# Two loading queues at the start of a fused attention and MLP block: other pieces, other order

## The chip, the cores and the metric

The kernel runs on one core of one Trainium2 chip. A core has five engines with a queue of instructions each: TensorE (PE) for matrix products, ScalarE (ACT), VectorE (DVE), GpSimd (POOL) and SyncE (SP). Transfers from memory are issued here by SP (queue q1 in the profile, "the sync queue") and by ACT (queue q10, "the scalar queue"). The metric is the time on the device in microseconds; lower is better. The median of five runs before the change is 158.0 us (157.48 to 158.24).

## The reference

All inputs are bf16. x has 2048 tokens of 448 features. The output is the sum of x, a linear attention of the normalised x, and a two-layer perceptron of the normalised x:

```python
xn  = layernorm(x)
qkv = (xn @ wqkv)                      # 16 heads of 28
phi = concat(softmax(q @ w_phi), softmax(-q @ w_phi))   # the same for k
kv  = phi_k^T v ;  z = sum over s of phi_k
o   = (phi_q kv) / (phi_q z + 1e-6)
out = x + o @ wo + silu(xn @ w1) @ w2  # w1: 448 x 1792, w2: 1792 x 448
```

## The kernel before, in words

The tokens are 16 tiles of 128, `t` 0 to 15, in four chunks of four tiles. `x_sb[:, t]` holds tile t. The contraction of 448 is cut into 7 slices of 64 rows, and every matrix product is issued as a pair on the lower and the upper half of PE's rows (`LO`, `HI`).

Every operation is first recorded in a list (`_Prog.op`, L167) with an estimated duration and the memory it reads and writes. A planner (`schedule`, L199; `_pass`, L229) then gives each engine its order. PE's order is the order of the program. Operations recorded with `ordered=True` also keep the program's order on their engine, and all loads are of that kind. The others are placed by estimated start and due time; `eng_free` (L254) says from when an engine is free. `emit_engine` (L961) writes the engines' instructions with semaphore waits, each engine working strictly through its list. So an instruction that waits holds up all behind it on its engine, and a transfer that waits holds up all transfers behind it on its queue.

The start goes as follows.

- POOL makes an identity matrix; PE multiplies it with itself (`warm`, L474), 32 + 4 pairs, before there is data. ACT loads its table for Silu with a dummy activation (L471).
- SP issues loads of x0, x1, the lower half of w1's first piece, x2 and x3 as one load, the lower halves of w1's second and third piece, then wqkv's columns for q and k (`wraw`, loads "wqk0" and "wqk1") and for v. ACT issues the upper halves of w1's three pieces and then four small loads of w_phi into `BD`. `load_w1` (L493) cuts w1 at columns 256, 512 and 896 of each half.
- Layernorm of a tile: statistics on DVE (`LN_st`, L533), aggregation on DVE and the power -1/2 on POOL (`LN_ag`, L538), the scaled copy `xnd` on DVE (`LN_b`, L547). Tiles 0 to 3 are then transposed on PE (`X_tr`, L572) and evicted to `xT`, one half by ACT and one by DVE (`X_ev`, L578). Tiles 4 to 11 are transposed by DMA transposes on the sync queue (`X_dma`, L562).
- `F1p` (L601) and `F1` (L589) are the first layer of the perceptron: a pair of 128-row tiles of the hidden layer, over 128 or more tokens, then Silu on ACT. Tile 0 and 1 start with `F1p`; then `F1(0, i, 0, 2)` for i from 2 to 6 does the other hidden tiles for tiles 0 and 1, with `X_tr` of tiles 2 and 3 in between, and `F1(0, i, 2, 2)` does all of them for tiles 2 and 3.
- `FT_tr` (L762) and `FM` (L785) multiply w_phi into the q and k weights on PE, from `wraw` and `BD`.
- `phase_e(0)` (L869) is then V and QK of the first chunk, with two second-layer tiles as fillers, `F2_early(f2[0])` and `F2_early(f2[1])`. After it, chunk 1's first layer, `F1(1, i, 0, 4)`, reads the transposes of tiles 4 to 7.
- Later loads carry `after=`, an instruction of PE that has to be over first. The loads of x8 to x11 and x12 to x15 wait for the end of `QK(0)`:

```python
QK(0)
mk = P.ops[P.last[("pe", "o")]]
QK(1)
F2_early(f2[0])
load_x(8, 12, after=mk)
load_x(12, 16, after=mk)
```

On the sync queue they come before the four transposes of tiles 4 to 7 (L567), and the first transpose of `phT` (L638) comes behind those.

Of the kernel before, what the change touches and what calls it, by code (L numbers as in the profile page):

```python
# [8 lines left out]
ACTF = mybir.ActivationFunctionType  # L9
# [129 lines left out]
class _Prog:  # L139
# [89 lines left out]
    def _pass(self, when):  # L229
        ops = self.ops  # L230
        n = len(ops)
        lat = self.lat
        tend = max(when.values()) + 3000.0
        for o in reversed(ops):
            if o.eng == "pe":
                o.alap = when[o.id]
                continue
            m = tend
            for u in o.users:
                uu = ops[u]  # L240
                if u in o.odeps:
                    continue
                m = min(m, uu.alap - (lat(o, uu) if o.id in uu.deps else 0.0))
            extra = 0.0
            if o.is_dma:
                extra = o.fixed if o.fixed is not None else 1200.0 + o.nbytes
            o.alap = m - o.dur - extra

        ndeps = [len(o.deps) + len(o.odeps) for o in ops]
        ready = {e: set() for e in ENGINES}  # L250
        for o in ops:
            if ndeps[o.id] == 0:
                ready[o.eng].add(o.id)
        eng_free = {"pe": 800.0, "act": 2100.0, "dve": 800.0, "pool": 800.0, "sp": 800.0}  # L254
        act_table = [None]
        dma_free = [0.0]
        order = {e: [] for e in ENGINES}
        done = 0
        WAIT_TOL = 60.0

        def est(o):
            t = eng_free[o.eng]
            for d in o.deps:
                dd = ops[d]
                t = max(t, dd.end + lat(dd, o))
            for d in o.odeps:
                t = max(t, ops[d].end if not ops[d].is_dma else ops[d].start + ops[d].dur)
            if o.eng == "act" and o.table is not None and act_table[0] is not None and o.table != act_table[0]:
                t += 1300.0
            return t  # L270

        while done < n:
            best = None
            for e in ENGINES:
                if not ready[e]:
                    continue
                c = [(est(ops[i]), ops[i]) for i in ready[e]]
                t0 = min(x[0] for x in c)
                t, o = min(((t, o) for t, o in c if t <= t0 + WAIT_TOL), key=lambda x: (x[1].alap, x[1].id))
                for t2, o2 in c:  # L280
                    if o2 is o or o2.alap >= o.alap or t2 >= t + o.dur:
                        continue
                    la = max(t - o.alap, t + o.dur - o2.alap, 0.0)
                    lb = max(t2 - o2.alap, t2 + o2.dur - o.alap, 0.0)
                    if lb < la - 1.0:
                        t, o = t2, o2
                if best is None or t < best[0]:
                    best = (t, o)
            assert best is not None, "scheduler deadlock"
            t, o = best  # L290
            ready[o.eng].discard(o.id)
            o.start = t
            if o.is_dma:
                issue_end = t + o.dur
                eng_free[o.eng] = issue_end
                if o.fixed is not None:
                    o.end = t + o.fixed
                else:
                    x0 = max(issue_end + 900.0, dma_free[0])
                    dma_free[0] = x0 + o.nbytes  # L300
                    o.end = dma_free[0] + 300.0
            else:
                o.end = t + o.dur
                eng_free[o.eng] = o.end + (0.0 if o.eng == "pe" else 30.0)
                if o.eng == "act" and o.table is not None:
                    act_table[0] = o.table
            order[o.eng].append(o.id)
            done += 1
            for u in o.users:
                ndeps[u] -= 1  # L310
                if ndeps[u] == 0:
                    ready[ops[u].eng].add(u)
        return order, max(o.end for o in ops)


def bass_parallel_sum__linear_kernel_hedgehog__dense_activation_silu__prompt_kernel(
# [21 lines left out]
    with es:  # L338
# [65 lines left out]
        P = _Prog()  # L404
# [54 lines left out]
        def load(dst, src, nbytes, run, name, eng="sp", issue=650.0, after=None):  # L459
            return P.dma(lambda e: e.dma_start(out=dst, in_=src), service(nbytes, run), writes=[dst], name=name, eng=eng,  # L460
                         issue=issue, ordered=True, after=after)
# [6 lines left out]
        P.op("pool", 230, lambda e: e.memset(ones_bf[:], 1.0), [], [ones_bf[:]], name="ones", ordered=True)  # L468
        P.op("pool", 290, lambda e: e.affine_select(ident[:], ones_bf[:], [[1, 128]], ALU.is_equal, 0.0, base=0,
                                                    channel_multiplier=-1), [ones_bf[:]], [ident[:]], name="ident", ordered=True)  # L470
        P.op("act", 220, lambda e: e.activation(tabw[:], neghalf[:], ACTF.Silu), [neghalf[:]], [tabw[:]],  # L471
             table="silu", name="tab", ordered=True)

        def warm(n, sl=2, d=55.5):  # L474
            for i in range(n):
                pair([(bank(2 * sl + q)[:, 0:128], ident[HALF[q], :], ident[HALF[q], :], True, True) for q in range(2)],
                     128, "warm", dur=d)

        P.unit = "warm"
        warm(32, d=107.0)  # L480
        warm(4)


        xv = A_x[0].rearrange("(p t) d -> p t d", t=NT)
        ov = out[0].rearrange("(p t) d -> p t d", t=NT)

        def load_x(t0, t1, after=None):
            load(x_sb[:, t0:t1, :], xv[:, t0:t1, :], (t1 - t0) * 128 * D * 2, (t1 - t0) * D * 2, f"x{t0}", issue=430, after=after)

        w1v = B_w1.rearrange("(s p) f -> p s f", p=64)  # L490
        W1S = [0, 256, 512, 896]
# [1 line left out]
        def load_w1(i):  # L493
# [2 lines left out]
            load(w1_sb[LO, :, a:b], w1v[:, :, a:b], n, (b - a) * 2, f"w1l{i}")  # L496
            load(w1_sb[HI, :, a:b], w1v[:, :, 896 + a:896 + b], n, (b - a) * 2, f"w1h{i}", eng="act")

        load_x(0, 1)
        load_x(1, 2)  # L500
        load_w1(0)
        load_x(2, 4)
        load_w1(1)
        load_w1(2)
        load(wraw[:, 0:3, 8:904], A_wqkv[0:384, 0:896].rearrange("(b p) c -> p b c", p=128), 384 * 896 * 2, 1792, "wqk0")
        load(wraw[LO, 3, 8:904], A_wqkv[384:448, 0:896], 64 * 896 * 2, 1792, "wqk1")
        P.op("pool", 300, lambda e: e.memset(BD[:], 0.0), [], [BD[:]], name="bd0", ordered=True)
        for p0 in (0, 904):
            P.op("pool", 150, lambda e, p0=p0: e.memset(wraw[:, :, p0:p0 + 8], 0.0), [], [wraw[:, :, p0:p0 + 8]],
# [23 lines left out]
        def LN_st(t, od=False):  # L533
            P.unit = f"LN{t}"
            xs = x_sb[:, t, :]
            P.op("dve", 630, lambda e: e.bn_stats(st6[:, t, :], xs), [xs], [st6[:, t, :]], name="bnst", ordered=od)  # L536
# [41 lines left out]
        def X_ev(t, sl, qs=(0, 1), od=False):  # L578
            P.unit = f"X{t}"
            j = t % 4  # L580
            for q in qs:
                src = bank16(2 * sl + q)[:, 0:448].rearrange("p (s n) -> p s n", s=NS)
                dst = xT[:, 0, :, j * 128 + q * 64:j * 128 + (q + 1) * 64]
                if q == 0:
                    act(dst, src, ACTF.Identity, 448, name="xT_ev")
                else:
                    P.op("dve", 390, lambda e, dst=dst, src=src: e.tensor_copy(dst, src), [src], [dst], name="xT_ev", ordered=od)  # L587
# [227 lines left out]
        X_tr(0, s0, HS, NS)  # L815
        X_ev(0, s0, (0, 1), True)
        LN_b(1, PARTS[1:], True)
        LN_st(2, True)
        P.unit = "warm"
        warm(10)  # L820
        give(s0)
# [1 line left out]
        def x1():  # L823
            X_tr(1, s1, 0, HS)
            X_tr(1, s1, HS, NS)
            X_ev(1, s1, (0, 1), True)
            LN_ag(2, True)
            LN_st(3, True)
            LN_ag(3, True)
            LN_b(2, od=True)  # L830
            LN_b(3, od=True)
            pads_init()
# [36 lines left out]
        def phase_e(c, f2):  # L869
            t = 4 * c  # L870
            if c == 0:
                V(0, lambda: FM(2))
                V(2, lambda: FM(3))
                QK(0)
                mk = P.ops[P.last[("pe", "o")]]
                QK(1)
                F2_early(f2[0])
                load_x(8, 12, after=mk)
                load_x(12, 16, after=mk)
                QK(2)  # L880
                QK(3)
                F2_early(f2[1])
                pend.extend((0, 1, 2, 3))
                return
            QK(t)
            mk = P.ops[P.last[("pe", "o")]]
            if c == 1:
                for s in range(NS):
                    for q in range(2):
                        load(wo_sb[HALF[q], s, :], wov[s], 64 * D * 2, 896, f"wo{s}", after=mk)  # L890
            F2_early(f2[0])
            QK(t + 1)
            V(t)
            kv(2)
            QK(t + 2)
            F2_early(f2[1])
            QK(t + 3)
            kv(2)
            V(t + 2)
            pend.extend((t, t + 1, t + 2, t + 3))  # L900
# [138 lines left out]
```

## Time and profile before

| | before |
|---|---|
| median of five runs | 158.0 us |
| the profiled execution, its own time | 157.97 us |
| its span in the profile | 156.2 us |
| PE busy (2298 matmuls) | 144.4 us, 92% of the span |
| DVE, ACT, POOL busy | 94.0, 93.4, 83.6 us |
| transfers of q1 (sync), q10 (scalar) | 15.44 and 0.83 MB |
| q8, "instruction" | 18 packets, 0.29 MB |
| first real matmul of the first layer | 8.4 us |

The profile gives each instruction's start and length, and for an engine that stood idle what ended the idle time. "issue" means that the engine waited for nothing that the profile shows. The chain of work that ended last is followed back from the last instruction; its lines are start, length, and what. In the views of transfers a queue's line gives packets, megabytes, and the time its packets took as a share of 16 transfer engines over the window asked for; packets are counted where they begin, so a share can be over 100%. In lines of work: start, length, engine, line, operation, output and input, and in brackets the idle time before it and its releaser.

### The profile page before, as it was taken

What the parts mean: (1) busy time and instruction counts of PE and PEld (TensorE: products, weight loads), DVE (VectorE), ACT (ScalarE), POOL (GpSimd) and SP (SyncE); (2) the same over time, 40 slices, a digit from 0 to 9 for tenths busy, and PEclk for the clock granted to TensorE, in tenths of its full rate; (3) what the DMA queues carried; (4) which work ended last, traced back from release to release, by engine and by line L of the source; (5) the groups of instructions that cost most, each with busy time, mean ns of one, the idle gap of its engine ahead of it and who ended that gap; (6) DMA issues with size and microseconds to landing.
All of it is one profiled execution on the core that took longest, in us unless ns stands there. A gap on an engine that the chain in (4) does not pass through costs nothing.

```text
span 156.2 us, 5256 instructions
## 1 busy us (share of the span) xinstructions
PE 144.4 (92%) x2298; PEld 91.4 (59%) x2298; DVE 94.0 (60%) x172; ACT 93.4 (60%) x120; POOL 83.6 (53%) x95
## 2 busy tenths in 40 slices
PE   6646979999899999999999999999999999999990
PEld 6535978555455555555555556565556666666650
DVE  2546118699997549790029697864036564955653
ACT  3035678898766877796689586678663324033330
POOL 2307000524989994959912899986993402222220
PEclk9999999999999999999999999999999999999999
DMA  4999993099160999377790023423080011111203
GB/s 113 224 192 265 218 365 111 4 260 190 27 69 4 176 193 102 89 111 143 162 170 15 0 67 72 71 65 74 7 181 18 4 73 51 63 61 42 84 0 117
DMA packets 37855, 16.60 MB, mean 106 GB/s; under 512 B 29192, under 2 KB 37576, under 8 KB 37832
## 3 DMA queue, kind: packets, MB, share of 16 engines
q1 hardware_dynamic: 35936, 15.44, 45.5%
q10 hardware_dynamic: 1896, 0.83, 2.9%
q8 instruction: 18, 0.29, 0.8%
q14 instruction: 5, 0.04, 0.1%
HBM read 7.48 MB, written 1.84 MB: 60 GB/s over the span
## 4 chain that ended last, share of the span: by engine, by line
PE 86%; DMA 8%; issue 2%; DVE 1%; SPq 1%; DVEq 0%
PE psum L429 84%; DMA x_sb<-in_A_x_dram 5%; DMA xT<-xnd 3%; PE psum L442 2%; SPq L460 1%; DVE Ye L687 0%; DVE st L536 0%; DVE x_sb L755 0%; DVEq L990 0%; DVE xT L587 0%; SPq L567 0%
## 5 line engine op out<-in xcount | busy, mean ns | idle before, releaser
L637 POOL TENSOR_TENSOR E<-E,Rk 128x896 bf16<-128x896 bf16 x32 | 53.4, 1697 | 10.9 <-ACT E L447 5.4
L429 PE MATMUL psum<-xT,w_sb 64*128 64x512 bf16 (+2 forms) x518 | 46.8, 324 | 5.2 <-issue 2.6
L429 PE MATMUL psum<-w_sb,hT 64*128 64x448 bf16 x448 | 45.2, 349 | 0.0
L447 ACT ACTIVATE hT<-psum 128x1024 bf16<-128x1024 f32 (+1 forms) x35 | 29.5, 852 | 14.4 <-PE psum L429 12.0
L429 PEld LDWEIGHTS psum<-xT,w_sb 64*128 64x128 bf16 x518 | 25.6, 94 | 19.2 <-issue 3.9
L429 PEld LDWEIGHTS psum<-w_sb,hT 64*128 64x128 bf16 x448 | 24.6, 94 | 16.6
L630 DVE TENSOR_REDUCE Sk<-E 128x64 f32<-128x1792 bf16 x16 | 31.8, 2004 | 2.8 <-ACT E L447 2.7
L447 ACT ACTIVATE E<-psum 128x896 bf16<-128x896 f32 x32 | 27.4, 917 | 6.2 <-PE psum L429 6.0
L447 ACT ACTIVATE xT<-psum 128x896 bf16<-128x896 bf16 (+2 forms) x20 | 13.0, 690 | 29.8 <-PE psum L442 26.3
L429 PE MATMUL psum<-wqk,xT 64*128 64x448 bf16 x224 | 23.6, 349 | 0.0
L701 POOL TENSOR_TENSOR xT<-xT,x_sb 128x448 f32<-128x448 f32 x8 | 8.3, 1033 | 24.9 <-ACT xT L447 22.4
L429 PEld LDWEIGHTS psum<-wqk,xT 64*128 64x128 bf16 x224 | 12.1, 94 | 8.7
L554 DVE TENSOR_SCALAR xnd<-x_sb,mv,rstd 128x896 bf16<-128x896 bf16 (+2 forms) x18 | 11.2, 656 | 9.3 <-POOL rstd L544 9.2
L544 POOL TENSOR_TENSOR rstd<-ve,neghalf 128x1 f32<-128x1 f32 x16 | 8.8, 563 | 9.5 <-DVE ve L542 9.1
L536 DVE BATCH_NORM_STATS2 st<-x_sb 128x6 f32<-128x448 bf16 x16 | 9.4, 609 | 6.5 <-DMA x_sb<-in_A_x_dram 6.5
L689 POOL TENSOR_TENSOR Ye<-Ye,x_sb 128x448 f32<-128x448 f32 x8 | 8.1, 1034 | 7.8 <-DVE Ye L687 7.8
L429 PE MATMUL psum<-wv_sb,xT 64*128 64x448 bf16 x112 | 12.1, 349 | 0.0
L429 PE MATMUL psum<-wo_sb,xT 64*128 64x448 bf16 x112 | 11.9, 349 | 0.0
L687 DVE TENSOR_TENSOR Ye<-psum,Ye 128x448 f32<-128x448 f32 x8 | 5.0, 621 | 9.7 <-ACT Ye L447 9.7
L726 DVE TENSOR_TENSOR xT<-psum,rden 128x224 bf16<-128x224 f32 x32 | 10.2, 382 | 0.2
L542 POOL TENSOR_SCALAR ve<-mv 128x1 f32<-128x1 f32 x12 | 2.3, 215 | 14.1 <-DVE mv L540 14.1
L755 DVE TENSOR_TENSOR x_sb<-psum,Ye 128x448 bf16<-128x448 f32 x8 | 4.6, 620 | 7.6 <-PE psum L429 7.6
(45 smaller groups left out, 110.6 us busy)
## 6 DMA issues: line engine op xcount, KB each, us to landing
out_dram<-x_sb SPq DMA_DIRECT2D x8, 224.0 KB, 1.9
w_sb<-in_B_w_dram SPq DMA_DIRECT2D x2, 784.0 KB, 6.7
x_sb<-in_A_x_dram SPq DMA_DIRECT2D x2, 448.0 KB, 4.1
wv_sb<-in_A_wqkv_dram SPq DMA_DIRECT2D x2, 392.0 KB, 13.5
wo_sb<-in_A_wo_dram SPq DMA_DIRECT2D x14, 56.0 KB, 2.2
x_sb<-in_A_x_dram SPq DMA_DIRECT2D x3, 224.0 KB, 7.0
phT<-in_A_wqkv_dram SPq DMA_DIRECT2D x1, 672.0 KB, 11.8
w_sb<-in_B_w_dram ACTq DMA_DIRECT2D x2, 224.0 KB, 4.5
```

Source lines behind the costliest of these rows:

```text
L429: ins = e.matmul(dst, lhsT, rhs, start=st, stop=sp, skip_group_check=True)
L447: return P.op("act", d_act(n), lambda e: e.activation(dst, src, func, scale=scale), reads=reads or [src], writes=writes or [dst], table=ta ...
L536: P.op("dve", 630, lambda e: e.bn_stats(st6[:, t, :], xs), [xs], [st6[:, t, :]], name="bnst", ordered=od)
L544: P.op("pool", 580, lambda e: e.tensor_tensor(rstd[:, t:t + 1], ve[:, t:t + 1], neghalf[:], ALU.pow), [ve[:, t:t + 1], neghalf[:]], [rstd[ ...
L554: lambda e, dst=dst, src=src: e.tensor_scalar(dst, src, mv[:, t, 0:1], rstd[:, t:t + 1], ALU.subtract, ALU.mult),
L630: dve(lambda e: e.tensor_reduce(Sk[:, t % 3, :].rearrange("p (h g) -> p h g", g=2), Er, AXL.X, ALU.add), d_dve(1792), [Er], [Sk[:, t % 3, ...
L637: pool(lambda e, Eh=Eh, Rb=Rb: e.tensor_tensor(Eh, Eh, Rb, ALU.mult), 1770, [Eh, Rh], [Eh], "phi%d" % qk)
L687: dve(lambda e: e.tensor_tensor(y, b, y, ALU.add), d_dve(D), [b, y], [y], "ye_d")
L689: pool(lambda e: e.tensor_tensor(y, y, x_sb[:, t, :], ALU.add), 1110, [y, x_sb[:, t, :]], [y], "ye_x")
L701: pool(lambda e: e.tensor_tensor(y, y, x_sb[:, t, :], ALU.add), 1110, [y, x_sb[:, t, :]], [y], "yl_x")
L726: dve(lambda e, dst=dst, src=src, rb=rb: e.tensor_tensor(dst, src, rb, ALU.mult), d_dve(224), [src, r], [dst], "o")
L755: dve(lambda e, b=b, y=y, dst=dst: e.tensor_tensor(dst, b, y, ALU.add), d_dve(D), [b, y], [dst], "out")
```

## The change

- The statistics of tile 2 (`LN_st(2)`) are recorded later: not after tile 0's eviction and tile 1's scaled copy, but after tile 1's eviction. As they are `ordered`, DVE runs them behind that eviction.
- x2 and x3 are loaded separately; `load_x` gets a parameter for its queue, which no call uses.
- wqk is loaded in three pieces: rows 0 to 255 on the sync queue, rows 256 to 383 and 384 to 447 on the scalar queue, behind w1's upper halves and ahead of the loads of `BD`. In the order that the planner gives ACT, one load of `BD` follows directly, two come behind the first eviction of xT, and one behind the first Silu.
- 38 warm pairs, not 32 + 4.
- The planner takes ACT as free from 800 and the table's dummy activation as 1500 ns long. On ACT the table load stays first, then w1's three pieces.
- x8 to x15 wait for the end of the second filler tile. On the sync queue they now stand behind the four transposes of tiles 4 to 7 and ahead of the first transpose of `phT`.
- In the planned order on POOL one residual addition (L689) moves from ahead of eight multiplications of `E` to behind them; on the sync queue two of the `wo` loads are issued a little later.

```diff
-        eng_free = {"pe": 800.0, "act": 2100.0, "dve": 800.0, "pool": 800.0, "sp": 800.0}
+        eng_free = {"pe": 800.0, "act": 800.0, "dve": 800.0, "pool": 800.0, "sp": 800.0}
...
-        P.op("act", 220, lambda e: e.activation(tabw[:], neghalf[:], ACTF.Silu), [neghalf[:]], [tabw[:]],
-             table="silu", name="tab", ordered=True)
...
-        warm(32, d=107.0)
-        warm(4)
+        warm(38, d=107.0)
...
+        P.op("act", 1500, lambda e: e.activation(tabw[:], neghalf[:], ACTF.Silu), [neghalf[:]], [tabw[:]],
+             table="silu", name="tab", ordered=True)
         load_x(0, 1)
         load_x(1, 2)
         load_w1(0)
-        load_x(2, 4)
+        load_x(2, 3)
+        load_x(3, 4)
         load_w1(1)
         load_w1(2)
-        load(wraw[:, 0:3, 8:904], A_wqkv[0:384, 0:896].rearrange("(b p) c -> p b c", p=128), 384 * 896 * 2, 1792, "wqk0")
-        load(wraw[LO, 3, 8:904], A_wqkv[384:448, 0:896], 64 * 896 * 2, 1792, "wqk1")
+        load(wraw[:, 0:2, 8:904], A_wqkv[0:256, 0:896].rearrange("(b p) c -> p b c", p=128), 256 * 896 * 2, 1792, "wqk0")
+        load(wraw[:, 2, 8:904], A_wqkv[256:384, 0:896], 128 * 896 * 2, 1792, "wqk1", eng="act")
+        load(wraw[LO, 3, 8:904], A_wqkv[384:448, 0:896], 64 * 896 * 2, 1792, "wqk2", eng="act")
...
         X_ev(0, s0, (0, 1), True)
         LN_b(1, PARTS[1:], True)
-        LN_st(2, True)
...
             X_ev(1, s1, (0, 1), True)
+            LN_st(2, True)
             LN_ag(2, True)
...
                 QK(0)
-                mk = P.ops[P.last[("pe", "o")]]
                 QK(1)
                 F2_early(f2[0])
-                load_x(8, 12, after=mk)
-                load_x(12, 16, after=mk)
                 QK(2)
                 QK(3)
                 F2_early(f2[1])
+                mk = P.ops[P.last[("pe", "o")]]
+                load_x(8, 12, after=mk)
+                load_x(12, 16, after=mk)
```

More of the change, by code (lines that the diff above doesn't have):

```diff
@@ L479, in bass_parallel_sum__linear_kernel_hedgehog__dense_activation_silu__prompt_kernel, with load_x @@
         P.unit = "warm"
-        warm(32, d=107.0)
-        warm(4)
+        warm(38, d=107.0)
         xv = A_x[0].rearrange("(p t) d -> p t d", t=NT)
         ov = out[0].rearrange("(p t) d -> p t d", t=NT)
-        def load_x(t0, t1, after=None):
-            load(x_sb[:, t0:t1, :], xv[:, t0:t1, :], (t1 - t0) * 128 * D * 2, (t1 - t0) * D * 2, f"x{t0}", issue=430, after=after)
+        def load_x(t0, t1, after=None, eng="sp"):
+            load(x_sb[:, t0:t1, :], xv[:, t0:t1, :], (t1 - t0) * 128 * D * 2, (t1 - t0) * D * 2, f"x{t0}", issue=430, after=after,
+                 eng=eng)
         w1v = B_w1.rearrange("(s p) f -> p s f", p=64)
```

## The prediction, made before the changed kernel had run

> **What bounds the kernel now.** I read the chain of work that ended last first, in order of time, because the change touches only the first 45 us and the question is which waits there are paid by the end. After 40.46 us TensorE (PE) runs without a hole in the chain to 152.62, so whatever moves the start of that run moves the end one for one, and nothing else in the change can.
>
> ```profile
> 2.48 7.92 DMA x_sb<-in_A_x_dram
> 10.40 0.02 issue
> 10.42 0.63 DVE st L536
> 11.05 0.30 DVE xT L587
> 11.35 0.05 issue
> 11.40 2.48 PE psum L429 x56
> 13.88 0.20 PE psum L442 x14
> 14.09 0.11 PE psum L429 x2
> 14.20 1.60 issue
> ...
> 20.36 0.65 PE psum L429 x12
> 21.01 0.96 issue
> ...
> 36.26 4.06 DMA xT<-xnd
> 40.32 0.14 issue
> 40.46 78.45 PE psum L429 x1030
> ```
>
> Four holes stand in it: VectorE (DVE) sits in `LN_st(2)` until the load of x2 and x3 lands at 10.40, and the xT eviction of tile 1, queued behind it, runs at 11.05 (PE idle 1.81 us before 11.40); 1.60 us and 0.96 us of "issue", in which PE waited for no engine and no load; and a wait for the transposes of tiles 4 to 7 up to 40.46. The two issue holes are code. Queue q8, "instruction", moves 18 packets of 16 KB, while PE runs 2298 weight loads and 2298 matmuls; between the two holes lie 12+14+56+32+12 = 126 matmuls, so 252 instructions and a few separate waits, about 256 of 64 bytes: one packet. The DMA view over narrow windows shows the packets themselves. These are the lines of 13 to 14 us, then of 19 to 20 us (packets, MB, share of the 16 engines):
>
> ```profile
> q1 hardware_dynamic: 214, 0.37, 101.4%
> q8 instruction: 1, 0.02, 7.0%
> ```
>
> ```profile
> q1 hardware_dynamic: 222, 0.22, 94.2%
> q8 instruction: 1, 0.02, 8.5%
> ```
>
> Narrowed further they begin at 13.2 to 13.3 and 19.1 to 19.2 and take 1.12 and 1.35 us; PE goes on 2.6 and 2.8 us after they began. The next two begin at 24.3 and 28.8, 2.4 us after PE resumed (21.97) or crossed the next block (some 126 matmuls later, near 26.4). With q1 busy it was 3.3 us (15.80 to 19.1). So a block is asked for when PE leaves the one before the last, and it is late by what stands in the DMA engines. The first late block was asked for about 7 us in (126 matmuls before the first hole) and came at 15.80.
>
> **The Trainium skill** (Runtime: NRT & Kernel Launch, Instruction fetch mechanics) has the same blocks of 16 KiB and 256 instructions and a queue of their own, but calls the cost of a crossing mostly hidden. The row disagrees: 1.60 + 0.96 us. By the rule, PE moved earlier is time won; by the row, PE is pinned at 15.80 and 21.97, however early it gets there. I take the row.
>
> **The change, part by part.**
>
> *`LN_st(2)` behind the eviction of tile 1.* ScalarE (ACT) evicts its half at 9.33 to 9.87, and DVE is free from 8.39, so DVE's half can run near 9.4 and tile 1's matmuls start at 9.9 and not 11.40. What is late next: `F1(0,2)` needs w1's second piece. The sync queue's half was issued at 3.3 and landed after 8.4 us, at 11.7. Its two tiles take 1.65 us, so PE reaches the transposes of tile 2 near 13.4 (before: 13.72), and there the code block ends. Of 1.5 us won, some 0.3 are left at 13.4 and none at 15.80. Counted: 0.
>
> *Four more warm matmuls.* 72 took 4.02 us, 56 ns each: 0.22 us more, ending at 5.7 where the first transpose starts at 6.91 (held by xnd), so the time is hidden. But their 8 instructions push every block border 4 matmuls earlier in the program. While PE resumes at fixed times (15.80, 21.97), it then has 4 matmuls more to do: at 55 ns (56 in 3.06 us) **+0.2 us**. If the code were never late this would be 0.
>
> *x2 and x3 apart.* One issue of 0.78 us becomes two of about 0.4 (as x0 and x1); runs of 896 bytes instead of 1792. x2 lands a little before 10.4. DVE now asks for it near 10, with PE idle until 11.7 anyway: 0.
>
> *wqk over both queues.* The sync queue loses an issue and 336 KB; the scalar queue gets two issues (0.52 and 0.63 us by the rows on the sync queue) and 192 rows of 1792 bytes ahead of the four BD loads, two of which now stand after the first eviction and one after the first Silu. ACT is idle up to 7.62 (5.33 us), which hides the issues; BD is read at 24.76, over 10 us later. The bytes are the price. After w1's upper half the scalar queue had little left; the lines of 9 to 10 us and of 12 to 13 us:
>
> ```profile
> q1 hardware_dynamic: 304, 0.16, 109.0%
> q10 hardware_dynamic: 123, 0.01, 18.7%
> ```
>
> ```profile
> q1 hardware_dynamic: 165, 0.27, 103.4%
> q10 hardware_dynamic: 40, 0.00, 4.1%
> ```
>
> Now 336 KB of wqk stand there beside w1's lower half and the code block. In the window 13 to 14 us the 214 packets of q1, nearly all wqk, took 101.4% of 16 engine-microseconds, 76 ns each; 192 of them are 14.6 engine-us, 0.9 us on each engine. The page DMA: Bandwidth & Descriptors (Issuing engines are not separate DMA queues) speaks against the change here: both queues run on the same 16 engines, so a second one saves issue time only. The row agrees, engines full from 4 us on (shares of 100 to 128%). So w1's last lower piece (4.0 + 9.4 = 13.4) goes to about 14.3, still ahead of 15.80, and the code block, whose packet began only when the scalar queue had run dry (4.1% in 12 to 13 us, none after), is behind 0.9 us more work. Cost between 0 (it gets its turn as before) and 2.4 (it waits until wqk and BD, sharing with q1, are all through, near 15.6). I take the service time, **+0.9 us**, nearest to the row of the same packets. The block after it is asked for on arrival and shifts with it; its 6.2 us I leave alone. FT_tr reads wqk at 19.7 (landed 16.4 and 17.0 before): covered by over 2 us.
>
> *Planner figures* (ACT free at 800 not 2100, table 1500 not 220): ACT's first items keep their order (table load, then w1's three pieces), so nothing moves on the chip but BD. A later residual add on GpSimd (POOL) moves behind eight multiplications; POOL then has 3.61 us idle before 82.27: 0.
>
> *x8 to x15 held to the end of the second filler tile.*
>
> ```profile
> 30.69 0.80 SPq L460 DMA_DIRECT2D x_sb<-in_A_x_dram  x2
> 31.54 6.02 SPq L567 DMA_TRANSPOSE xT<-xnd  x4
> 41.89 1.24 SPq L638 DMA_TRANSPOSE phT<-E  x1
> ```
>
> ```profile
> 37.11 2.82 PE L429 MATMUL psum<-w_sb,hT 64*128 64x448 bf16 x28
> 40.46 1.90 PE L429 MATMUL psum<-xT,w_sb 64*128 64x512 bf16 x16 [0.53 <-DMA xT<-xnd]
> ```
>
> The 896 KB went out 0.8 us ahead of the four transposes on the same queue; the transposes landed 5.0, 4.4, 4.6 and 4.1 us after their issue, the last at 40.32, where the median of all twelve is 3.2 and the shortest issue 1.22 us. Without the loads, the fourth is issued near 35.2 (31.4 + 3 x 1.27) and lands near 38.4, before the filler tile ends at 39.93: **-0.5 us**, the whole hole. Bounds 0 and -0.53. Behind the held loads on the sync queue stands only the first phT transpose, which waits for POOL until 41.89 anyway; it now follows 896 KB (2.5 us), and its reader is at 115 us, the next writer of that E buffer near 60 us. x8 lands at 39.9 + 3.7 = 43.6 and x12 near 44.5; DVE wants them at 44.35 and 46.69. Cover 0.7 us; if it is gone, DVE's statistics and POOL's rstd slip, with transposes that PE reads at 65.18.
>
> **The sum**, on the profiled execution (157.97 us, span 156.2 and 1.8 around it; the median shown is 158.0): 157.97 + 0.2 + 0.9 - 0.5 = **158.6 us**.
>
> **Rivals.**
> *A, code block on time as before (about the same).* The turn of the scalar queue costs the code packet nothing, or less than 0.77: 157.7 to 158.4. For it: the block came while q1 alone was full, too, and the work as a whole is the same, only on two queues. Against: nothing else explains why the first block took twice as long as the second.
> *B, the start is not pinned (faster).* The code packet follows PE's progress more closely than I think, or lighter work on q1 lets it pass sooner. Then the 1.60 us hole shrinks by up to what PE gains, bounded by w1's second and third pieces (11.7, 13.4): 0.5 to 1.3 us. 157.97 - 0.5 - 0.6 = 156.9. It decides as soon as the block arrives 0.2 us earlier than 15.80. Against: the request stands about 7 us in, before anything that the change moves.
> *C, the clock (slower still).* PE now stops near 13.5 instead of 14.2. If the block comes after 16.9, PE has stood 3.4 us, the idle time after which the page TensorE: Matmul & The Clock Gate (Part 1) has the clock halved; no stall here was that long and the granted clock was 1.00 throughout. 3.4 us at half speed lose 1.7, of which the next hole hides 1.0: 159.5 and more.
> *D, the hole at 40.46 stays,* because something else is late there: 159.1. Against: ACT's last exponentials end at 39.34, and the next accumulator is free.
>
> **Numbers.** The measured times spread over 0.5%, so about 0.3% (0.47 us) is what can be told from no change. Slower 0.45: my sum 0.35, C 0.06, D 0.04. A 0.27. B 0.28. Slower's own range is 158.5 to 160; 8 in 10 must take in A and the nearer half of B, so 157.0 to 159.9.
>
> **What would show it.** LN_st(2)'s wait gone and tile 1's matmuls near 9.9; the first issue hole longer than 2 us and ending near 16.7, with q10 carrying 1792-byte packets until then; 4 matmuls more after each hole; no wait on the transposes at 40. I am wrong if the instruction packet begins before 13.3, or if the w1 pieces and not code release PE.

## The result, and the profile after

The changed kernel is a little slower: 1.0041 times the time before, with a 95% interval of 1.0023 to 1.0059. That is 0.65 us (0.36 to 0.94). The plain medians, 158.96 and 158.58 us, also hold some disturbed executions, which the ratio leaves out. The profiled execution took 158.70 us (span 157.0) against 157.97 (span 156.2), 0.73 us more.

The chain of work that ended last, of the changed kernel (start, length, what):

```profile
9.77 0.97 PE psum L429 x28
10.76 0.61 ACT hT L447
11.37 1.44 issue
12.80 3.17 PE psum L429 x28
15.98 0.23 PE psum L442 x13
16.20 1.11 issue
17.32 0.20 PE psum L442
...
24.13 16.43 PE psum L429 x238
40.59 0.55 ACT Ye L447
41.14 0.06 issue
41.20 78.46 PE psum L429 x1030
```

DVE no longer sits in `LN_st(2)` ahead of the eviction: tile 1's products start at 9.77 (11.40 before). Then PE stands until 12.80. The chain calls that "issue", but what landed there is w1's second lower piece: issued at 3.8, 8.9 us on the way, 12.7 (before 3.3 + 8.4 = 11.7). The two parts of wqk on the scalar queue, which PE doesn't read before 21.4, had landed at 10.8 and 11.6, ahead of it. The 28 matmuls that follow took 3.17 us, 113 ns each, where they took 1.53 us, 55 ns each, before. PE then stops for code, behind the 13th of tile 2's 14 transposes, and goes on at 17.32, 1.5 us later than before (15.80, three matmuls further in the program). The second code hole, 0.96 us at 21.01, is gone: PE is now later than its block. So only 0.74 us are left at 41.20, and the run from there to the last filler is as long as before (78.46 against 78.45).

The granted clock of the changed kernel by stretch (PE, PEld, DVE, ACT and POOL busy, then PEclk, DMA share and GB/s):

```profile
12.00:13.00 1.00, 0.20 (x4) 0.19 (x5) 0.98 (x3) 0.00 (x0) 0.86 (x3) 0.76 1.13 204
13.00:14.00 1.00, 1.00 (x12) 0.85 (x10) 0.46 (x1) 0.00 (x0) 1.00 (x5) 0.50 1.07 211
16.00:17.00 1.00, 0.20 (x13) 0.08 (x6) 0.00 (x0) 0.60 (x1) 0.00 (x0) 1.00 1.13 235
```

The transfers of the changed kernel in the windows 11 to 12 and 14 to 15 us (packets, MB, share of the 16 engines); narrower windows put the start of the code packet at 14.60, where it was 13.25 before:

```profile
q1 hardware_dynamic: 279, 0.20, 113.4%
q10 hardware_dynamic: 1, 0.00, 0.1%
```

```profile
q1 hardware_dynamic: 226, 0.28, 93.4%
q10 hardware_dynamic: 179, 0.01, 14.9%
q8 instruction: 1, 0.02, 7.4%
```

So the code packet did not stand behind wqk on the scalar queue: that queue is all but empty from 11 to 13 us, and what it carries from 13 on are the small packets of `BD`.

The timelines of SP's queue and of PE around the held loads:

```profile
32.00 5.34 SPq L568 DMA_TRANSPOSE xT<-xnd  x4
40.58 0.81 SPq L460 DMA_DIRECT2D x_sb<-in_A_x_dram  x2
42.64 1.24 SPq L639 DMA_TRANSPOSE phT<-E  x1
```

```profile
37.73 2.82 PE L429 MATMUL psum<-w_sb,hT 64*128 64x448 bf16 x28
41.20 1.04 PE L429 MATMUL psum<-xT,w_sb 64*128 64x512 bf16 x8 [0.65 <-ACT Ye L447]
```

The loads of x8 to x15 are out of the transposes' way, as planned, and the hole ahead of the first matmul on tiles 4 to 7 is not closed: 0.65 us, 0.53 before. The bracket names ACT; but the last transpose, issued at 36.05, took 5.0 us, to 41.06, and that is what the matmul needed. The first three took 3.1 us each, where they took 5.0, 4.4 and 4.6 us with the loads ahead of them.

### The profile page after: what moved, and what is told of

Its sections match the earlier page's. It is cut to its first block, busy times and chain, and to the rows that moved or that the text cites. A ratio compares the mean times of both kernels' runs of the same rounds, so it can differ in the third digit from the quotient of the medians.

```text
span 157.0 us, 5263 instructions
## 1 busy us (share of the span) xinstructions
PE 146.2 (93%) x2302; PEld 94.4 (60%) x2302; DVE 94.3 (60%) x172; ACT 93.4 (60%) x120; POOL 83.5 (53%) x95
## 4 chain that ended last, share of the span: by engine, by line
PE 90%; DMA 3%; issue 2%; DVE 2%; ACT 1%; POOL 0%; DVEq 0%; SPq 0%
PE psum L429 87%; DMA x_sb<-in_A_x_dram 3%; PE psum L442 2%; DVE xnd L555 1%; POOL rstd L545 0%; DVE st L537 0%; DVE x_sb L756 0%; ACT hT L447 0%; ACT Ye L447 0%; ACT xT L447 0%; DVEq L991 0%; SPq L460 0%; DVE xT L588 0%; DVE mv L541 0%; DVE ve L543 0%
## 5 line engine op out<-in xcount | busy, mean ns | idle before, releaser
L638 POOL TENSOR_TENSOR E<-E,Rk 128x896 bf16<-128x896 bf16 x32 | 53.3, 1697 | 10.1 <-DVE Rk L633 6.9
L429 PE MATMUL psum<-xT,w_sb 64*128 64x512 bf16 (+2 forms) x518 | 48.0, 332 | 3.4 <-issue 2.1
L429 PEld LDWEIGHTS psum<-xT,w_sb 64*128 64x128 bf16 x518 | 26.9, 96 | 17.1 <-issue 2.7
L688 DVE TENSOR_TENSOR Ye<-psum,Ye 128x448 f32<-128x448 f32 x8 | 5.0, 621 | 11.7 <-ACT Ye L447 6.6
```

The costliest lines, as they stand in the source:

```text
L429: ins = e.matmul(dst, lhsT, rhs, start=st, stop=sp, skip_group_check=True)
L638: pool(lambda e, Eh=Eh, Rb=Rb: e.tensor_tensor(Eh, Eh, Rb, ALU.mult), 1770, [Eh, Rh], [Eh], "phi%d" % qk)
L688: dve(lambda e: e.tensor_tensor(y, b, y, ALU.add), d_dve(D), [b, y], [y], "ye_d")
```

## The experiments

"Theory 1" in the expectations is the prediction's main term: the 336 KB of wqk on the scalar queue make the first code packet late. Each text names its rivals. All ratios are to the kernel before, measured on the same chip.

### wqk back on the sync queue

```diff
-        load(wraw[:, 0:2, 8:904], A_wqkv[0:256, 0:896]..., "wqk0")
-        load(wraw[:, 2, 8:904], A_wqkv[256:384, 0:896], ..., "wqk1", eng="act")
-        load(wraw[LO, 3, 8:904], A_wqkv[384:448, 0:896], ..., "wqk2", eng="act")
+        load(wraw[:, 0:3, 8:904], A_wqkv[0:384, 0:896]..., "wqk0")
+        load(wraw[LO, 3, 8:904], A_wqkv[384:448, 0:896], ..., "wqk1")
```

> The changed kernel with wqk back on the sync queue alone (two pieces as before). Theory 1 (the 336 KB on the scalar queue stand ahead of PE's code block): the late code packet begins near 13.3 us instead of 14.6, PE leaves the code hole near 15.8 instead of 17.3, and the time is 0.9 us under the changed kernel's, ratio to the kernel before about 0.998. Theory 2 (PE's clock is halved because it stands still after tile 1's first products): w1's second piece lands near 11.7, the stand is about 1 us, the granted clock stays 1.00; the gain is the same or larger, so this run alone doesn't tell the two apart. Rival 3 (the queue doesn't matter, the packet is late by chance): packet and time as in the changed kernel, ratio 1.004.

Measured: 0.9989 (0.9955 to 1.0022), first code packet at 12.90. Without the split the loss is gone. The planner had moved the four loads of `BD` on the scalar queue as well, so it was done again with the planned order frozen:

```diff
         order = P.schedule(5500.0)
         ops = P.ops
+        late = [i for i in order["act"] if ops[i].name in ("wqk1", "wqk2")]
+        order["act"] = [i for i in order["act"] if i not in late]
+        at = [ops[i].name for i in order["sp"]].index("wqk0") + 1
+        order["sp"][at:at] = late
```

> The changed kernel with its two wqk parts of 336 KB moved from the scalar queue to the sync queue, right behind the first wqk part, after the planner has run: the order of every other instruction is the changed kernel's. In the earlier kernel without the split the planner had also put later VectorE, GpSimd and DMA steps in another order; here only the queue differs. Theory 1 (wqk on the scalar queue stands in front of PE's code packet, 0.9 us): ratio 0.996 to 0.999 to the kernel before, first code packet at 12.8 to 13.4, w1's second piece in time for matmuls at 11.4. Theory 2 (the loss comes from the later steps, which the planner moved): 1.003 to 1.005 as the changed kernel, although the packet comes early.

(The text says that the planner had moved later VectorE, GpSimd and DMA steps in the earlier kernel. Laid side by side, the two kernels differ in the place of `BD`'s loads and in two wqk parts instead of one, so they are nearly repeats.) Measured: 1.0002 (0.9975 to 1.0030), code packet at 13.21. Theory 2 falls. All other parts of the change together are worth nothing that can be told from zero. Its chain:

```profile
9.81 3.12 PE psum L429 x70
12.93 0.34 PE psum L442 x13
13.28 2.50 issue
15.78 0.20 PE psum L442
```

This is the prediction's pinned start, alone on view. PE runs without a stop from 9.81 and reaches tile 2's transposes at 12.93, where the kernel before starts them at 13.88; then it waits 2.50 us and goes on at 15.78; the kernel before went on at 15.80, three matmuls further.

### The split alone

The kernel before, with wqk cut in three and two parts put on the scalar queue behind w1's last piece after planning, all else in its place:

```diff
         order = P.schedule(5500.0)
         ops = P.ops
+        part = [i for i in order["sp"] if ops[i].name in ("wqk1", "wqk2")]
+        order["sp"] = [i for i in order["sp"] if i not in part]
+        at = [ops[i].name for i in order["act"]].index("w1h2") + 1
+        order["act"][at:at] = part
```

> The kernel before with nothing but wqk's split: two parts of 336 KB on the scalar queue behind w1's upper half, put there after the planner has run, so that no other instruction changes place. Theory 1: first code packet at 14.0 to 14.8 (13.25 before), w1's second lower piece after 12.3, ratio 1.004 to 1.007. Theory 2: packet unchanged within 0.3 us or its lateness hidden, ratio 0.998 to 1.002.

Measured: 1.0045 (1.0020 to 1.0071), 0.7 us (0.3 to 1.1): as much as the whole loss, from this edit alone. But the first code packet began at 13.21, as in the kernel before. The price came in elsewhere. Its chain, and the instruction on DVE that leads it:

```profile
12.55 0.96 PE psum L429 x28
13.51 0.08 issue
13.59 2.96 PE psum L429 x28
16.55 0.37 PE psum L442 x14
16.92 0.99 PE psum L429 x14
```

```profile
11.49 0.63 DVE L537 BATCH_NORM_STATS2 st<-x_sb 128x6 f32<-128x448 bf16 x1 [3.31 <-DMA x_sb<-in_A_x_dram]
```

x2 and x3 landed 1.06 us later (11.46 against 10.40), `LN_st(2)`, still ahead of the eviction here, waited 3.31 us, and tile 1 started at 12.55 (11.40 before). With a half clock from 13.9 to 17, PE reached the block border at 16.9, when its code had been there for about 1 us, if it took the 2.55 us from packet to PE that it took before (13.25 to 15.80). At full clock the 28 matmuls would have taken 1.5 us and not 2.96, and PE would have been at the border near 15.3 (an estimate from these rows), before its code. So in this one profile it is the half clock, which set in 1.3 us after the end of a stand of 2.25 us, that makes PE late at the border; what part it has over all executions, no run here tells. What the split delays for certain is the sync queue. The issue rows of w1's third lower piece (336 KB on the sync queue; the last number is us from issue to landing) of the kernel before, the changed one, the one with the split undone, the split alone, and (below) all of wqk on the scalar queue:

```profile
w_sb<-in_B_w_dram SPq DMA_DIRECT2D x1, 336.0 KB, 9.4
```

```profile
w_sb<-in_B_w_dram SPq DMA_DIRECT2D x1, 336.0 KB, 10.1
```

```profile
w_sb<-in_B_w_dram SPq DMA_DIRECT2D x1, 336.0 KB, 8.5
```

```profile
w_sb<-in_B_w_dram SPq DMA_DIRECT2D x1, 336.0 KB, 11.8
```

```profile
w_sb<-in_B_w_dram SPq DMA_DIRECT2D x1, 336.0 KB, 12.1
```

Over all profiles the sets do not overlap: 8.5 to 9.4 us in seven kernels without wqk on the scalar queue, 10.1 to 11.8 in six with two parts of it there. Nor do they for w1's second piece, on which PE waits first: it landed at 11.1 to 11.7 us in the seven and at 12.6 to 13.5 in the six. The code packet is less clean: it began at 12.90 to 13.76 in five kernels without wqk on the scalar queue (those with wide warm matmuls left out, as their blocks lie elsewhere), and at 13.21, 13.50, 14.19, 14.48 and 14.60 in five with two parts there, the latter three 0.4 to 0.8 us behind the latest of the former. PE's restart behind it (the same point of the program in each) is at 15.9 to 16.5 without, and 16.4 to 17.7 with.

### All of wqk on the scalar queue

```diff
-        load(wraw[:, 0:2, 8:904], A_wqkv[0:256, 0:896]..., "wqk0")
+        load(wraw[:, 0:2, 8:904], A_wqkv[0:256, 0:896]..., "wqk0", eng="act")
```

> The changed kernel with all of wqk (784 KB) on the scalar queue, not 336 KB of it. Some later items on DVE, POOL and the sync queue are planned in another order. Theory 1: 1.2 us more of service stand ahead of the code packet; it begins after 15 us, and the time is 1 us over the changed kernel's (ratio 1.010). Rival (the queue gives the code its turn whatever stands there): the packet begins by 14.6 and the ratio is 1.004.

Measured: 1.0166 (1.0117 to 1.0214). More bytes, more loss; but again not by the code packet, which began at 13.11. Here PE waited for w1:

```profile
12.18 2.59 issue
14.77 3.17 PE psum L429 x28
```

The piece was issued at 3.81 and landed 10.9 us later, at 14.7; the matmuls that need it start at 14.77 (12.80 in the changed kernel, with 336 KB on the scalar queue; 11.24 and 11.40 in the two with the split undone). The planner also put some later steps in another order in this kernel, and holes appear at 36.7 and later (1.78 us of issue), so the size of its loss is not the price of the bytes alone.

### The hold

The kernel before with `load_x(8, 12)` and `load_x(12, 16)` behind `F2_early(f2[1])`, as in the change, and nothing else:

```diff
                 QK(0)
-                mk = P.ops[P.last[("pe", "o")]]
                 QK(1)
                 F2_early(f2[0])
-                load_x(8, 12, after=mk)
-                load_x(12, 16, after=mk)
                 QK(2)
                 QK(3)
                 F2_early(f2[1])
+                mk = P.ops[P.last[("pe", "o")]]
+                load_x(8, 12, after=mk)
+                load_x(12, 16, after=mk)
```

> The kernel before with nothing but the hold: x8 to x15 are issued behind the four transposes of tiles 4 to 7 and not ahead of them; no other instruction changes place. The prediction's step (the hole of 0.53 us before 40.46 closes): ratio 0.9955 to 0.998, the first matmul on tiles 4 to 7 at 40.0 or earlier. Rival D (one transfer engine is held by the 16 KB code packet that begins near 37.5, so that the last transpose lands late with or without x8 to x15): 0.9985 to 1.0015, a wait of 0.3 to 0.7 us stays before the first matmul on tiles 4 to 7.

Measured: 0.9998 (0.9966 to 1.0029). The reverse, the changed kernel with the loads released after `QK(0)` again and placed as before:

```diff
                 QK(0)
+                mk = P.ops[P.last[("pe", "o")]]
                 QK(1)
                 F2_early(f2[0])
+                load_x(8, 12, after=mk)
+                load_x(12, 16, after=mk)
...
                 F2_early(f2[1])
-                mk = P.ops[P.last[("pe", "o")]]
-                load_x(8, 12, after=mk)
-                load_x(12, 16, after=mk)
```

> The changed kernel with x8 to x15 released after QK(0) again, ahead of the four transposes of tiles 4 to 7. The prediction: holding them was worth 0.5 us, so this is 0.5 us slower than the changed kernel (ratio 1.007). Rival (the last transpose is held up by a packet of code on its transfer engine, whatever stands ahead of it): the hole ahead of chunk 1's first layer stays 0.5 to 0.7 us and the ratio stays at 1.004.

Measured: 1.0031 (0.9997 to 1.0065), where the changed kernel has 1.0041. The hold is worth nothing measurable. Why, the transfers of the hold-alone kernel say, in the windows 38 to 39 and 39 to 40 us:

```profile
q1 hardware_dynamic: 787, 0.20, 103.5%
q8 instruction: 1, 0.02, 5.9%
```

```profile
q14 instruction: 1, 0.01, 7.3%
q1 hardware_dynamic: 27, 0.00, 4.5%
```

A block border lies just inside the second filler tile (PE crosses it at 38.4). The code packet begins at 38.70; of the transposes' packets 787 begin in that microsecond and 27 in the next, with the engines nearly idle (4.5%), and the last transpose lands 4.6 us after its issue, at 41.1, where the median transpose takes 3.1. The changed kernel shows the same: packet at 38.63 for 1.25 us, the last transpose at 41.06. That the code packet holds one transfer engine, as the expectation has it, is not shown, as these traces name no engine; the delay is. A kernel of the section on fewer instructions sets loads and packet apart: the one before with wide warm matmuls still has the loads ahead of the transposes, but its code packet begins only at 41.55. Its four transposes took 4.9, 4.3, 3.2 and 3.1 us, and PE did not wait. So the loads slow the first two, and the packet slows the last, for which PE waits.

When that packet begins decides how much is waited. Take the start of the filler tile's last 14 matmuls as the mark, and as the wait what is over the shortest time from there to the first matmul on tiles 4 to 7, 1.32 us, in eleven kernels (the wide ones and the one with all of wqk on the scalar queue left out). Packet 1.2 to 1.6 us ahead of the mark: waits of 0 to 0.07 us (four kernels, all with the hold). Packet 0.4 to 0.95 us ahead: 0.36 to 0.86 us (seven; the three without the hold 0.68 to 0.71, four with it 0.36, 0.41, 0.82 and 0.86). So the hold doesn't close the hole. That it helps a little when the packet comes early is not excluded; in the times nothing of it is seen.

### The warm pairs

The changed kernel with 36 pairs instead of 38, and then the same with the split undone too, in the frozen order:

```diff
-        warm(38, d=107.0)
+        warm(36, d=107.0)
```

> The changed kernel with 36 warm pairs, not 38. The prediction: 8 instructions fewer move the border of PE's code blocks 4 matmuls later, worth 0.2 us (ratio 1.003). Rival: nothing, the warm products are hidden (ratio 1.004).

Measured: 1.0013 (0.9987 to 1.0040).

> The changed kernel with both of the parts undone that seem to cost: wqk on the sync queue alone, in the order of the changed kernel, and 36 warm pairs as before. What is left is LN_st(2) behind the eviction, the x split and the hold. Theory 1 with the 0.2 us of the warm pairs: 0.994 to 0.998, faster than both kernels. Rival (the start is pinned by the code packet, and LN_st(2) and the hold are worth nothing): 0.998 to 1.001.

Measured: 1.0004 (0.9979 to 1.0028), beside 1.0002 for 38 pairs in the same batch. The borders move as predicted, back to two matmuls into the product, and the second hole returns (0.47 us at 21.1). No time follows from it: with 38 pairs PE is 0.6 us later at 27 us, and waits 0.4 us less at 40. No kernel here is measurably faster than the one before.

### `LN_st(2)` back in front

The planner moves a few later steps on DVE, GpSimd and SyncE with it.

```diff
         LN_b(1, PARTS[1:], True)
+        LN_st(2, True)
...
             X_ev(1, s1, (0, 1), True)
-            LN_st(2, True)
```

> The changed kernel with LN_st(2) back ahead of tile 1's eviction on DVE. The prediction counted the move as 0, since PE is stopped later by w1's second piece and by code: ratio stays at 1.004, tile 1's first-layer products start near 10.9 and not 9.8. Theory 2 (clock): PE then has no stand of 2 us between tile 1's products and the next, the granted clock stays 1.00 in 12 to 16 us, and the time falls by some 0.5 to 1.5 us (ratio 0.995 to 1.001). Rival 3 (the move won its 1.5 us and something else lost more): 1.0 to 1.5 us slower, ratio 1.011 to 1.014.

Measured: 1.0004 (0.9976 to 1.0033). Tile 1 starts later and PE still waits, 2.34 us at 14.59, for a code packet that began at 14.19. Moving `LN_st(2)` bought nothing. Six kernels have two parts of wqk on the scalar queue: 1.0045 and 1.0041 stand beside 1.0031, 1.0013, 1.0011 and 1.0004, and only the first two are clear of 1. The intervals of this kernel and of the changed one overlap by little (up to 1.0033, from 1.0023). The four with the split undone or never made, narrow warm matmuls throughout, lie at 0.9989 to 1.0004. So the sign of the split's price is told; its size, between about 0 and 0.7 us, is not, and the parts do not add up better than 0.3% here.

### The clock

The changed kernel with PE kept busy while it waits for w1: eight pairs of 512 columns behind tile 1's products, and 3 + 27 pairs for the 38 at the start, so that the count of instructions ahead of the next border stays. The planner moves a few later steps here too.

```diff
-        warm(38, d=107.0)
+        warm4(3)
+        warm(27, d=107.0)
...
         F1p(1, 0)
+        warm4(8, sl=1, d=216.0)
```

> The changed kernel with PE kept busy where it stands after tile 1's first products: eight pairs of 512 columns (about 1.7 us) go there, and the warm products at the start are three wide pairs and 27 narrow ones, so the number of instructions, and with it the borders of the code blocks, stay. Theory 2 (the half clock behind that stand is what the change costs): granted clock 1.00 in 12 to 16 us and 0.5 to 1.5 us faster than the changed kernel, ratio 0.995 to 1.001. Theory 1 (code pins PE): the hole ends where it did, ratio stays near 1.004.

Measured: 1.0011 (0.9985 to 1.0036), which doesn't tell the theories apart; clock 0.999 in the profile. There the clock stayed up, the packet began at 14.41, and PE went on at 17.05 (17.32 in the changed kernel). So in these two profiles, with the code packet late, the half clock lies under its cover and costs 0.3 us at most. The time says less: in 15 of this kernel's 22 executions the clock still fell. The half clock is also no mark of the change: most executions of every kernel show it, the kernel before included, once or twice, for 3.4 us each (mean clock 0.988 for the changed kernel, 0.987 for the one before beside the first four experiments); the profile of before happened to have none. It goes with the time, but not by its length: in each of three batches the executions of the kernel before with one such stretch (told by their mean clock) took 0.9 to 1.0 us longer on the mean than those with none, and those with two only 0.1 to 0.4 us longer. Which is cause and which effect stays open.

### Fewer instructions

If borders pin the start, fewer instructions ahead of them should free it. The kernel before with 9 warm pairs of 512 columns in place of 36 of 128, and the changed kernel with 9 wide and 2 narrow ones and the split undone:

```diff
-        warm(32, d=107.0)
-        warm(4)
+        warm4(9)
```

```diff
-        warm(38, d=107.0)
+        warm4(9)
+        warm(2, d=107.0)
```

> The kernel before with 9 warm pairs of 512 columns for 36 of 128: PE is busy as long, with 108 instructions fewer, so every border of a code block falls 54 matmuls later in the program. Theory 1 (PE is pinned by the arrival of code): the hole at 14.2 us is gone or shorter, since PE reaches the border 2 to 3 us later; 1.0 to 2.5 us faster than the kernel before, ratio 0.984 to 0.994. Rival (the issue holes have another cause, tied to the place in the program): holes at the same matmuls, ratio 1.000.

> The changed kernel with wqk back on the sync queue and 9 wide warm pairs and two narrow ones for 38 narrow ones. Theory 1: both costs of code are met, 1.5 to 3 us faster than the kernel before, ratio 0.981 to 0.991. If w1's pieces and not code were the bound, the same as wqk back alone, 0.999.

Measured: 1.0039 (1.0008 to 1.0070) and 1.0057 (1.0003 to 1.0110): slower, the opposite. The chain of the first:

```profile
16.43 1.65 PE psum L429 x27
18.08 1.14 issue
19.22 1.83 PE psum L429 x29
```

The border lies 54 matmuls later in the work, and so does the border before it, which PE now crosses at 10.84 and not at 7.6. The packet began at 16.50, 5.65 us after that crossing; in the kernel before it was 5.63, in the split-undone kernel 5.57. The hole moved with the border. In the second kernel the next packet came 6.2 us after its crossing and cost 3.53 us. What counts is the time from one crossing to the next against the packet's way, not where the borders lie.

## Why the prediction was right in size and partly wrong in its reasons

Predicted 158.6, +0.6 us; measured +0.65 (0.36 to 0.94). The sum came out because two terms that failed, +0.2 and -0.5, and one that was somewhat too large, +0.9, nearly cancel; so that it came out this close is in part luck.

- *`LN_st(2)` behind the eviction, counted 0*: right, and by the mechanism given. The row at 9.81 of the split-undone kernel shows 1 us won at 12.9 and none at 15.78.
- *Four more warm matmuls, +0.2*: not confirmed. The borders moved by four; 1.0004 against 1.0002 (each about 0.27% either way) shows no price, though 0.2 us (0.13%) is below what the runs tell. The step that failed is to count on fixed resume times to the end: the wait at 40 takes up what was lost at 27.
- *wqk over both queues, +0.9*: right in sign. 0.7 us (0.3 to 1.1) for the split alone, and nothing left without it, though four other kernels with the split lost 0.1 to 0.5 us, none of them clear of zero. The place was only half right. The packet did begin later in the changed kernel (14.60), but not because it "is behind 0.9 us more work" on the scalar queue: the last of wqk's packets there had landed at 11.6, 3 us before. In the split-alone kernel it was not later, and there the sync queue's own loads set the time. The other step that failed is what was said of that queue. "w1's last lower piece goes to about 14.3" came out (14.51; the mean of its way went from 9.0 us in seven profiles to 10.5 in six), but the second piece was left at 11.7, and it came at 12.7 and held PE for 2.06 us; in the split-alone kernel x2 and x3 came later too (11.46 against 10.40). The cited rule (DMA: Bandwidth & Descriptors, Issuing engines are not separate DMA queues) points the same way and not far enough: the second queue did not just save nothing, it took the engines' time from loads that were needed first.
- *x8 to x15 held, -0.5*: wrong; rival D. The slow landings of 4.1 to 5.0 us were all read as the loads' work. Of the first two, which had landed by 37.34, that was so: with the hold they take 3.1 us. The last one, which PE waits for, was held up by the code packet that began at 37.49, and with the hold it still took 4.2 to 5.0 us in the six kernels where a packet began 2 us or more before it landed.
- *The second block, which "is asked for on arrival and shifts with" the first*: it did not shift. Its packet began at 19.14 (19.12 before), and as PE came 1.5 us later to its border, the hole of 0.96 us was gone. Behind the first hole the same matmul is 1.74 us late, behind the second 0.61: more was lost than predicted, and most of it paid back.
- *Rival C, the clock*: it was halved in the changed kernel, but within a stand of 2.06 us and while waiting for w1, not after 3.4 us on code, and at hardly any price in that profile; in the split-alone profile it was not covered.
- *The signs that it named*: tile 1's matmuls came as said (9.77). The hole on code was 1.11 us and ended at 17.32, not over 2 us and near 16.7, as PE first waited for w1's piece; "if the w1 pieces and not code release PE" was one of its signs of being wrong, and of the first wait it is so.
- *Rival A, the packet on time*: seen in the split-alone kernel, which was slower by 0.7 us (0.3 to 1.1) all the same.

Left open: what sets the code packet's turn. It took 5.2 to 7.3 us from the crossing in the first phase, and neither the scalar queue's bytes (784 KB: 6.0 us; 336 KB: 5.6 to 7.3; none: 5.2 to 6.4) nor its running dry orders these numbers.

## What to carry to other kernels

When the transfer engines are full, moving a load to a second queue is a change of priority: bytes not needed yet then take turns with those that are, so put on the second queue only what is needed as early as its neighbours (here two parts of wqk landed 10 us before their use, and w1's second piece 1 us later than before). A wait on a transfer needs the packets of all queues in that window, the instruction queue's too, before it is put down to the load beside it. And a hole at a code border is not closed by reaching it sooner or by moving it: look at the time between two crossings.

## What the runs showed of the hardware that was not expected

- A 16 KB code packet of 0.93 to 1.45 us, met by the transposes of tiles 4 to 7: the last of them took 4.1 to 5.0 us to land, where the median of all is 3.1 to 3.2, in nine kernels. Of the five in which the packet began less than 0.4 us before it landed, or later, four show 3.0 to 3.1 us and one, with all of wqk on the scalar queue, 3.6.
- PE's first code packet took 5.2 to 7.3 us from the crossing of the border before while the loads ran, and 0.7 to 2.2 us near 28 us, with the engines nearly idle (the kernels with wide warm matmuls left out). Blocks whose work is shorter than that way stop PE while the loads run, against the rule of the Trainium skill (Runtime: NRT & Kernel Launch, Instruction fetch mechanics) that the crossing is mostly hidden.
- The clock was halved for 3.41 us at a time, sometimes twice in a row, and within a trace its changes lie at multiples of 3.41 us from each other. Cut from there into windows of that length, the traces show, behind 9 us, a half clock after each window in which PE was busy for 39% of the time or less (nine kernels; 37% in the changed one, with its stand of 2.06 us). The stands of 1.81 and 1.60 us of the kernel before lie in two windows with 47% and 53%, and the clock stayed at 1.00. So in these traces the busy share of a fixed window tells the cases apart, and the length of one stand does not. Ahead of 9 us windows with 43 to 53% were followed by a half clock too (four kernels), which stays open. The 3.4 us of idle time that the Trainium skill gives (TensorE: Matmul & The Clock Gate, Part 1) were not reached by the stand in the changed kernel.
